# The head of a four-layer kernel: first row tile centred only for its v products, second row's statistics on ScalarE, norms interleaved, buffers cleared later on GpSimd

## The chip, the cores and the metric

One Trainium2 chip, one of its cores. The time is the device time of one execution in microseconds, and the median over runs is what counts. A core has five engines with instruction queues of their own: TensorE (PE, with a separate path for weight loads, PEld), VectorE (DVE), ScalarE (ACT), GpSimd (POOL) and SyncE (SP), which mostly issues transfers. Each runs its own queue in order and waits on semaphores for the others. Row tiles of 128 rows lie across the partitions; TensorE writes to PSUM, and VectorE or ScalarE copies from there to SBUF ("evacuates").

## The reference

Four layers A, B, A, B on x of 2048 x 576 in bf16, each with a residual. Only the first layer's beginning is touched by the change.

```python
def _layernorm(x, axis=-1, eps=1e-05):
    m = jnp.mean(x, axis=axis, keepdims=True)
    v = jnp.var(x, axis=axis, keepdims=True)
    return (x - m) / jnp.sqrt(v + eps)

def _A_ref(x, wqkv, wo):
    qkv = (x @ wqkv).reshape(B, S, 3, H, Dh).transpose(2, 0, 3, 1, 4)
    q, k, v = qkv[0], qkv[1], qkv[2]
    ...
    logits = jnp.einsum('bhsd,bhswd->bhsw', q, kg) * scale
    attn = _softmax(logits, axis=-1)
    o = jnp.einsum('bhsw,bhswd->bhsd', attn, vg)
    return o.transpose(0, 2, 1, 3).reshape(B, S, D) @ wo

x = x + _A_ref(_layernorm(x), A_wqkv, A_wo)
x = x + _B_ref(_layernorm(x), B_w_in, B_w_sp, B_b_sp, B_w_out)
...
```

## The kernel before, in words

The kernel runs the layers in turn (`build_kernel`). In layer A the engines' orders are written out by hand (`tc.manual_schedule` over PE, ACT, DVE, POOL and SP): the order of the Python statements is each engine's queue.

The first layer has a head of its own (`li == 0`, from line 676). Rows are taken in a permuted order (`rows_of`: first even rows, then odd), in 16 row tiles, here called rows 0 to 15.

- Loads (lines 687 to 693): row 0 on SP's queue, row 1 on ScalarE's, rows 2 and 3 on SP's, then the weights for v (`wv_sb`), rows 4 to 7, the weights for q and k (`wqk_sb`), rows 8 to 11. `exp_table` loads ScalarE's table for the exponential.
- Warm-up: 46 matmuls of a 128x128 identity with itself (L699).
- `build_window_rows` makes constant rows that give the attention window. It returns four pieces: `part0` (VectorE: bits of the row numbers), `pads` (GpSimd clears `win_pat`), `part1` (VectorE, and two transfers to DRAM), `part2` (GpSimd: four small operations and one transfer to DRAM). `load_pat` brings the pattern back from DRAM (four transfers on SP), and `fill_window_rows` spreads it over QK (VectorE, L201 and L204).
- Line 703 writes a column of ones into `v_ext` on ScalarE (each head has 18 values of v and a 1, from which the softmax's denominator comes). `setup_bufs` clears the last columns of four exponential buffers `P_sb` and four output buffers `o_t` on GpSimd (L434, L436).

A row tile's norm consists of `B_` (two `bn_stats` on VectorE, L715), `G_` (`bn_aggr`: mean and variance, L718), `R_` (VectorE adds epsilon, L727; GpSimd raises to -0.5, L728) and `A_` (VectorE: subtract the mean, multiply by the reciprocal deviation, into one of four buffers `ln_xn` taken in turn, L735). For rows 0 to 3 `T_pe` transposes the normed tile on TensorE (five transposes of 128x128 into a PSUM tile `pt`, L742), and ScalarE copies it into `xnT` (L745; in two pieces for row 0). From row 4 on, `T_` lets SP issue a transposing transfer instead.

`VW(t, hh, dve)` computes half a row tile of v: five matmuls into a PSUM tile `pv` (L451) and an evacuation into `v_ext` (L443 on VectorE, L445 on ScalarE). The v tiles are those of the attention: tile 0 has rows 0 to 127 of the permuted order, tile t begins 8 rows before its 120 queries, so that tile 1 needs the last 8 columns of row tile 0 in `xnT` and all but a few of row tile 1. Below, "(t, h)" is half h of tile t.

The head's order on TensorE is: warm-up, transposes of row 0, (0,0), row 1, (0,1), row 2, (1,0), (1,1), (2,0), row 3, (2,1), (3,0), (3,1); on VectorE the statistics of row i + 1 stand ahead of the norm of row i. The loop that writes this out:

```python
S_(0)
R_(0, 1)
for i in range(3):
    B_(i + 1)
    A_(i)
    G_(i + 1)
    R_(i + 1, 1)
    T_pe(i)
    for t, hh in (((0, 0),), ((0, 1),), ((1, 0), (1, 1)))[i]:
        VW(t, hh, False)
```

Then the q/k products follow (`PG`, `PG_mm`, L462): for each 128 columns d of q or k and each 512 rows cc, five matmuls of 512 columns, evacuated by ScalarE into `stg` buffers; once a buffer is complete, transfers on GpSimd's and SP's queues scatter it over QK by heads (L78). The ten (d, cc) with cc = 0 and 1 come first, cc = 1 needing rows 4 to 7. After them come (4,0) to (7,1) of v, eight more q/k products, and between these the first score group (`L_mm(0)`, L536) with its exponentials (`EXP`, L545).

PSUM tiles of these kinds are taken in turn from five places (`PT_tile`, two tagged Y and three PT); a tile's place must have been evacuated before it is taken again.

Of the kernel before, what the change touches and what calls it, by code (L numbers as in the profile page):

```python
# [9 lines left out]
ACT = mybir.ActivationFunctionType  # L10
ALU = mybir.AluOpType
AX = mybir.AxisListType
f32 = mybir.dt.float32
# [5 lines left out]
P = 128  # L19
D = 576  # L20
H = 32
DH = 18
# [4 lines left out]
EPS = 1e-5  # L27
# [36 lines left out]
class K:  # L64
# [316 lines left out]
    def layer_A(self, li):  # L381
        nc, tc, cfg = self.nc, self.tc, self.cfg
        S, NT, XW, NS = cfg.S, cfg.NT, cfg.XW, cfg.NS
        scale = float(DH ** -0.5)
# [43 lines left out]
        def k0_(t):  # L428
            return cfg.tiles[t][2]


        def setup_bufs(eng):
            for pb in P_bufs:
                eng.memset(pb[:, :, :, QT:P], 1.0)  # L434
            for ob_ in o_bufs:
                eng.memset(ob_[:, D:640], 0.0)  # L436
# [4 lines left out]
        def evac(out, in_, dve):  # L441
            if dve:
                nc.vector.tensor_copy(out=out, in_=in_)  # L443
            else:
                nc.scalar.copy(out=out, in_=in_)  # L445

        def VW(t, hh, dve):
            nk = tdim(t)[0]
            pv = self.PT_tile([P, 512], f32, "pv")
            for c in range(5):  # L450
                nc.tensor.matmul(pv[:nk, 0:288], lhsT=self.xnT[:, c, k0_(t):k0_(t) + nk],  # L451
                                 rhs=wv_sb[:, c, hh * 288:(hh + 1) * 288], start=(c == 0), stop=(c == 4))
            evac(v_ext[:nk, t, 16 * hh:16 * hh + 16, 0:DH], pv[:nk, 0:288].rearrange("p (b d) -> p b d", d=DH), dve)

        stg_tiles, stg_left = {}, {}
        dma_rr, stg_rr = [0], [0]
# [219 lines left out]
        if li == 0:  # L676
# [18 lines left out]
            self.zero_right()  # L695
            self.make_ident()
            warm = self.PT_tile([P, 512], f32, "warm")
            for _ in range(46):
                nc.tensor.matmul(warm[:, 0:P], lhsT=self.ident[:], rhs=self.ident[:], start=True, stop=True)  # L699
# [3 lines left out]
            nc.scalar.copy(out=v_ext[:, :, :, DH:DH + 1], in_=self.ones[:, None, None, :].to_broadcast([P, NT, H, 1]))  # L703
            rows[0]()
            rows[1]()
            setup_bufs(nc.gpsimd)
            mvs = sb.tile([P, NS, 2], f32, name="lnx_mv", tag="lnx_mv", bufs=1)
            rstds = sb.tile([P, NS], f32, name="lnx_rstd", tag="lnx_rstd", bufs=1)

# [2 lines left out]
            def B_(i):  # L712
                sts[i] = st = sb.tile([P, 2, nc.vector.BN_STATS_DIM], f32, name="ln_st", tag="ln_st", bufs=3)
                for s in range(2):
                    nc.vector.bn_stats(out=st[:, s, :], in_=xts[i][:, s * 288:(s + 1) * 288])  # L715

            def G_(i):
                nc.vector.bn_aggr(out=mvs[:, i, :], in_=sts.pop(i)[:])  # L718

            def S_(*tiles):  # L720
                for i in tiles:
                    B_(i)
                    G_(i)

            def R_(i0, n):
                rs = rstds[:, i0:i0 + n]
                nc.vector.tensor_scalar_add(out=rs, in0=mvs[:, i0:i0 + n, 1], scalar1=EPS)  # L727
                nc.gpsimd.tensor_tensor(out=rs, in0=rs, in1=self.neg_half[:, 0:1].to_broadcast([P, n]), op=ALU.pow)  # L728
            xns = {}

            def A_(*tiles):
# [3 lines left out]
                    nc.vector.tensor_scalar(out=xn[:, 0:D], in0=xts[i], scalar1=mvs[:, i, 0:1],  # L735
                                            scalar2=rstds[:, i:i + 1], op0=ALU.subtract, op1=ALU.mult)

            def T_pe(i):
                xn = xns.pop(i)
                pt = self.PT_tile([P, 5, P], bf16, "pt")  # L740
                for c in range(5):
                    nc.tensor.transpose(pt[:, c, :], xn[:, c * P:(c + 1) * P], self.ident[:])  # L742
                r = i * P
                for c0, c1 in ((0, 3), (3, 5)) if i == 0 else ((0, 5),):
                    nc.scalar.copy(out=self.xnT[:, c0:c1, r:r + P], in_=pt[:, c0:c1])  # L745

            def T_(*tiles):
                for i in tiles:
                    self.ln_T(xns.pop(i), i * P, P)
            S_(0)  # L750
            R_(0, 1)
            for i in range(3):
                B_(i + 1)
                A_(i)
                G_(i + 1)
                R_(i + 1, 1)
                T_pe(i)
                for t, hh in (((0, 0),), ((0, 1),), ((1, 0), (1, 1)))[i]:
                    VW(t, hh, False)
            rows[2](nc.sync)  # L760
            A_(3)
            VW(2, 0, False)
            T_pe(3)
            VW(2, 1, False)
            VW(3, 0, False)
            VW(3, 1, False)
            x3 = sb.tile([P, 4, D], bf16, name="x_in3", tag="x_in", bufs=2)
            x_load(x3[:], 12, 4, nc.sync)
            stgs.append(x3[:].rearrange("p a b -> p (a b)")[:, 0:2 * CBW].rearrange("p (a b) -> p a b", a=2))
# [12 lines left out]
            R_(8, 4)  # L782
            S_(12)
            A_(8, 9, 10, 11)
            T_(8, 9, 10, 11)
# [483 lines left out]
```

## Time and profile before

| | us |
|---|---|
| median of 3 runs | 1152.9 (1152.79 to 1153.15) |
| profiled execution | 1152.74, of which its span is 1150.9 |
| TensorE busy | 1142.6 (99% of the span) |
| VectorE, ScalarE, GpSimd busy | 539.7, 370.5, 259.6 |
| first warm-up matmul starts | 1.36 |
| first transposes of a normed row start | 6.00 |
| first v product starts | 7.03 |
| first q/k product starts | 13.42 |

How to read the lines below. A line of a timeline gives start, length, engine, line, operation, output <- input, shapes and count, and in brackets the idle time before it with what released it; instructions of a kind that follow each other are merged. A line of the chain gives start, length and what ran in the chain that ended last. A line of the groups gives count, busy time and mean length in ns, then the idle time before them. A line of a stretch gives its bounds and length, then busy time and count of PE, PEld, DVE, ACT and POOL, the granted clock, the share of the DMA engines and GB/s. In a list of transfer queues stand packets, MB and share.

### The profile page before, as it was taken

Reading aid. Unit: us, or ns where it says so; the run is one execution under the profiler, and the core shown is the slowest. Engines: PE = TensorE matmul, PEld = TensorE weight load, DVE = VectorE, ACT = ScalarE, POOL = GpSimd, SP = SyncE. Lnnn points to the kernel's source line nnn. Section 1 sums busy time; section 2 is a strip of 40 time slices with the busy share of each in tenths; the row PEclk is TensorE's granted clock in tenths of the full one; section 3 lists DMA queues with packets and bytes.
Section 4 is the critical chain, followed back from the end, with each engine's and each line's share of the span. In section 5 each row is a group of like instructions: output and inputs, shape, how many; then the busy total and the mean of one; then the engine's idle time right before and its main releaser. Section 6 shows DMA issues by size and latency. Waiting matters only on the chain.

```text
span 1150.9 us, 29693 instructions
## 1 busy us (share of the span) xinstructions
PE 1142.6 (99%) x12930; PEld 614.5 (53%) x12949; DVE 539.7 (47%) x1198; ACT 370.5 (32%) x660; POOL 259.6 (23%) x387
## 2 busy tenths in 40 slices
PE   8999999999999999999999999999999999999998
PEld 5567554444444444457755775544444444444676
DVE  8789987312233222244466889843322223222312
ACT  5589565011111111102247876541111111011000
POOL 3689654000000000002153767530000000000000
PEclk9999999999999999999999999999999999999999
DMA  8877696000000000049455867920000000001322
GB/s 195 183 164 200 141 211 137 10 13 13 13 1 13 13 13 2 1 152 213 110 110 110 180 152 176 246 60 1 13 13 13 13 13 1 13 2 30 101 74 58
DMA packets 177372, 91.26 MB, mean 79 GB/s; under 512 B 128788, under 2 KB 170420, under 8 KB 177242
## 3 DMA queue, kind: packets, MB, share of 16 engines
q1 hardware_dynamic: 164762, 70.75, 28.1%
q0 software_dynamic: 5888, 12.72, 4.6%
q10 hardware_dynamic: 6592, 5.90, 1.7%
q8 instruction: 101, 1.65, 0.6%
q14 instruction: 29, 0.24, 0.1%
HBM read 35.46 MB, written 14.69 MB: 44 GB/s over the span
## 4 chain that ended last, share of the span: by engine, by line
PE 97%; ACT 1%; DVE 1%; issue 0%; DVEq 0%; ACTq 0%
PE hh L234 79%; PE pp L462 6%; PE pv L451 3%; PE pw L629 3%; PE O_ps L559 3%; PE L_ps L536 2%; ACT P_sb L545 1%; PE L_ps L462 1%; PE hh L1191 0%; PE pt L595 0%; DVE ln_st L715 0%; DVE ln_xn L735 0%; DVE win_bits L158 0%; ACT v_ext L445 0%; ACT xnT L745 0%
## 5 line engine op out<-in xcount | busy, mean ns | idle before, releaser
L234 PE MATMUL hh<-Wq,Z 64*128 64x512 bf16 x4608 | 505.8, 376 | 0.0
L234 PEld LDWEIGHTS <-Z 64*128 64x128 bf16 x6984 | 339.8, 94 | 310.1
L1095 DVE TENSOR_TENSOR g_tmp<-hh,ln_xn 128x512 f32<-128x512 f32 x144 | 92.8, 686 | 452.3 <-PE hh L234 452.3
L947 ACT COPY bank_turn<-ones 1x1 bf16<-1x1 bf16 x239 | 44.8, 188 | 538.5 <-PE hh L234 538.5
L78 POOL DMA_DIRECT2D wout<-in_B_w_out_dram x4 | 4.3, 1075 | 602.0 <-PE hh L234 602.0
L234 PE MATMUL hh<-wout,Z 64*128 64x288 bf16 x2232 | 137.0, 283 | 0.0
L545 ACT ACTIVATE P_sb<-L_ps 128x1440 bf16<-128x1440 f32 (+3 forms) x136 | 125.0, 971 | 24.6 <-PE L_ps L536 23.2
L234 PE MATMUL hh<-xnT,w 64*128 64x512 bf16 x1152 | 132.2, 376 | 0.0
L234 PE MATMUL hh<-win2a,xnT 64*128 64x512 bf16 (+1 forms) x960 | 118.7, 355 | 0.0
L234 PEld LDWEIGHTS <-xnT 64*128 64x128 bf16 x1440 | 69.9, 94 | 70.0 <-issue 0.5
L1020 DVE BATCH_NORM_STATS2 z_st<-zp 128x6 f32<-128x512 bf16 (+1 forms) x160 | 93.0, 624 | 13.0 <-ACT zp L1018 12.9
L1086 ACT ACTIVATE z1T<-hh 128x1024 bf16<-128x1024 f32 x72 | 73.7, 1024 | 61.9 <-PE hh L234 61.9
L234 PEld LDWEIGHTS <-w 64*128 64x128 bf16 x1152 | 56.1, 94 | 68.3
L1096 DVE TENSOR_TENSOR Z<-g_tmp,z1T 128x512 bf16<-128x512 f32 x144 | 92.4, 683 | 0.0
L1018 ACT ACTIVATE zp<-hh 128x1024 bf16<-128x1024 f32 (+1 forms) x96 | 76.1, 810 | 48.8 <-PE hh L234 48.6
L462 PE MATMUL pp<-xnT,wqk_sb 128*128 128x512 bf16 (+1 forms) x313 | 74.2, 379 | 0.9
L234 PE MATMUL hh<-win2b,xnT 64*128 64x512 bf16 (+1 forms) x480 | 72.8, 355 | 0.0
L1160 DVE TENSOR_TENSOR x_new<-hh,xo 128x288 bf16<-128x288 f32 x64 | 26.3, 453 | 93.0 <-PE hh L234 85.0
L299 POOL TENSOR_SCALAR ln_xn<-x_new,ln_mv,ln_rstd 128x576 bf16<-128x576 bf16 x28 | 64.2, 2293 | 2.7
L78 POOL DMA_DIRECT2D QK<-stg x76 | 48.0, 636 | 36.5 <-DVE stg L443 21.9
L462 PEld LDWEIGHTS <-wqk_sb 128*128 128x128 bf16 (+1 forms) x360 | 32.1, 97 | 36.6 <-issue 1.9
L1044 POOL TENSOR_SCALAR Z<-zp,z_mv,z_rstd 128x256 bf16<-128x256 bf16 x32 | 50.7, 1584 | 3.5
(124 smaller groups left out, 753.3 us busy)
## 6 DMA issues: line engine op xcount, KB each, us to landing
xres<-x_new SPq DMA_DIRECT2D x44, 144.0 KB
wout<-in_B_w_out_dram POOLq DMA_DIRECT2D x4, 1296.0 KB, 7.4
xo<-xres SPq DMA_DIRECT2D x32, 144.0 KB
xn_rows<-ln_xn SPq DMA_DIRECT2D x28, 160.0 KB
w<-in_B_w_in_dram SPq DMA_DIRECT2D x16, 256.0 KB
QK<-stg POOLq DMA_DIRECT2D x51, 72.0 KB, 4.4
QK<-stg SPq DMA_DIRECT2D x37, 72.0 KB
xo<-in_A_x_dram SPq DMA_DIRECT2D x6, 288.0 KB
```

The lines of the kernel that those rows point to most:

```text
L78: return eng.dma_start(out=out, in_=in_)
L234: ins = self.nc.tensor.matmul(outs[a_], lhsT=lhs(a_, c, r0), rhs=rhs(a_, c, r0), start=start and k_ == 0, stop=stop and k_ == len(chunks) ...
L299: e.tensor_scalar(out=xn[:nrows, 0:D], in0=x_t[:nrows, :], scalar1=mv[:nrows, 0:1], scalar2=rstd[:nrows, 0:1], op0=ALU.subtract, op1=ALU.mult)
L462: nc.tensor.matmul(pp, lhsT=w, rhs=self.xnT[r0:r1, c, cc * 512:(cc + 1) * 512], start=start, stop=stop, tile_position=(r0, 0))
L545: nc.scalar.activation(out=P_bufs[2 * jp + s % 2][:nk, :, :, 0:nq], in_=Lv[:nk, :, :, 0:nq], func=ACT.Exp, scale=scale)
L947: self.turn_on = lambda tok: nc.scalar.copy(out=tok, in_=self.ones[0:1, 0:1])
L1018: nc.scalar.activation(out=zp[:, w0:w0 + n], in_=pz, func=ACT.Gelu_apprx_tanh)
L1020: nc.vector.bn_stats(out=st[:, x // 512, :], in_=zp[:, x:x + min(512, w0 + n - x)])
L1044: eng.tensor_scalar(out=Z[:, b0:b1, i, :], in0=zv[:, b0:b1, :], scalar1=mv[:, 0:1], scalar2=rstd[:, 0:1], op0=ALU.subtract, op1=ALU.mult)
L1086: lambda ht, z1T=z1T, q2=q2: nc.scalar.activation(out=z1T[:, q2 * 512:(q2 + 2) * 512], in_=ht[:].rearrange("p a b -> p (a b)"), func=ACT.G ...
L1095: nc.vector.tensor_tensor(out=tmp[:], in0=pg[:, a_, :], in1=bsp[:, qs], op=ALU.add)
L1096: nc.vector.tensor_tensor(out=uT(jj)[:, sub, qs], in0=tmp[:], in1=z1Ts[jj, sub][:, qs], op=ALU.mult)
```

## The change

- Warm-up of 40 instead of 46 matmuls.
- Row 0: VectorE writes the centred row (mean subtracted, not scaled) into `ln_xn` 0 (`xc`). It is transposed, copied in two pieces into `o_slot` 0 (`xcT`), and both halves of v's tile 0 are computed from it; ScalarE's evacuation multiplies by row 0's reciprocal deviation (`scaled`). Afterwards row 0 is normed, transposed and copied to `xnT` as before, first its last 8 columns, then the other 120 (`T_out`).
- Row 1's statistics: two passes on ScalarE (sum; sum of squares of the differences from the mean), GpSimd computes mean, variance and power. VectorE's `bn_stats` and `bn_aggr` of row 1 are gone.
- The order on TensorE becomes: warm-up, centred row 0, (0,0), row 0, row 1, (0,1), (1,0), row 2, (1,1), (2,0), row 3, (2,1), (3,0), (3,1). ScalarE copies row 3 (and row 2) before it evacuates (2,0) (and (1,0)).
- `pads` moves on GpSimd behind the power of row 2, `part2` ahead of the powers of rows 4 to 7. The ones in `v_ext` and `setup_bufs` move behind the power of rows 8 to 11, the ones from ScalarE to GpSimd.
- The statistics of row 6 move ahead of the norms of rows 4 and 5 on VectorE, those of row 8 ahead of the norms of rows 6 and 7.

```diff
-        def VW(t, hh, dve):
+        def VW_mm(t, hh, xT=None):
             nk = tdim(t)[0]
             pv = self.PT_tile([P, 512], f32, "pv")
             for c in range(5):
-                nc.tensor.matmul(pv[:nk, 0:288], lhsT=self.xnT[:, c, k0_(t):k0_(t) + nk],
+                nc.tensor.matmul(pv[:nk, 0:288], lhsT=self.xnT[:, c, k0_(t):k0_(t) + nk] if xT is None else xT[:, c, 0:nk],
                                  rhs=wv_sb[:, c, hh * 288:(hh + 1) * 288], start=(c == 0), stop=(c == 4))
-            evac(v_ext[:nk, t, 16 * hh:16 * hh + 16, 0:DH], pv[:nk, 0:288].rearrange("p (b d) -> p b d", d=DH), dve)
+            return v_ext[:nk, t, 16 * hh:16 * hh + 16, 0:DH], pv[:nk, 0:288].rearrange("p (b d) -> p b d", d=DH)
+
+        def VW(t, hh, dve):
+            evac(*VW_mm(t, hh), dve)
...
-            for _ in range(46):
+            for _ in range(40):
...
-            nc.scalar.copy(out=v_ext[:, :, :, DH:DH + 1], in_=self.ones[:, None, None, :].to_broadcast([P, NT, H, 1]))
             rows[0]()
-            rows[1]()
-            setup_bufs(nc.gpsimd)
...
+            def E_(i0, n):
+                nc.vector.tensor_scalar_add(out=rstds[:, i0:i0 + n], in0=mvs[:, i0:i0 + n, 1], scalar1=EPS)
+
+            def W_(i0, n):
+                rs = rstds[:, i0:i0 + n]
+                nc.gpsimd.tensor_tensor(out=rs, in0=rs, in1=self.neg_half[:, 0:1].to_broadcast([P, n]), op=ALU.pow)
+
             def R_(i0, n):
...
+                E_(i0, n)
+                W_(i0, n)
...
-            def T_pe(i):
-                xn = xns.pop(i)
+            def T_mm(xn):
                 pt = self.PT_tile([P, 5, P], bf16, "pt")
                 for c in range(5):
                     nc.tensor.transpose(pt[:, c, :], xn[:, c * P:(c + 1) * P], self.ident[:])
-                r = i * P
-                for c0, c1 in ((0, 3), (3, 5)) if i == 0 else ((0, 5),):
-                    nc.scalar.copy(out=self.xnT[:, c0:c1, r:r + P], in_=pt[:, c0:c1])
+                return pt
+
+            def T_out(i, pt, c0=0, c1=5, r0=0, r1=P):
+                nc.scalar.copy(out=self.xnT[:, c0:c1, i * P + r0:i * P + r1], in_=pt[:, c0:c1, r0:r1])
...
+            def scaled(out, in_):
+                nc.scalar.activation(out=out, in_=in_, func=ACT.Identity, scale=rstds[:, 0:1])
+            sums = sb.tile([P, 2], f32, name="lnx_sum", tag="lnx_sum", bufs=1)
+            spill = self.xn_bufs[1][:, 0:D]
+            nc.scalar.activation(out=spill, in_=xts[1], func=ACT.Identity, accum_out=sums[:, 0:1])
+            nc.gpsimd.tensor_scalar(out=mvs[:, 1, 0:1], in0=sums[:, 0:1], scalar1=1.0 / D, scalar2=None, op0=ALU.mult)
+            nc.scalar.activation(out=spill, in_=xts[1], func=ACT.Square, scale=-1.0, bias=mvs[:, 1, 0:1],
+                                 accum_out=sums[:, 1:2])
             S_(0)
-            R_(0, 1)
-            for i in range(3):
-                B_(i + 1)
-                A_(i)
-                G_(i + 1)
-                R_(i + 1, 1)
-                T_pe(i)
-                for t, hh in (((0, 0),), ((0, 1),), ((1, 0), (1, 1)))[i]:
-                    VW(t, hh, False)
-            rows[2](nc.sync)
-            A_(3)
-            VW(2, 0, False)
-            T_pe(3)
-            VW(2, 1, False)
+            E_(0, 1)
+            xc = self.xn_bufs[0]
+            nc.vector.tensor_scalar(out=xc[:, 0:D], in0=xts[0], scalar1=mvs[:, 0, 0:1], scalar2=None, op0=ALU.subtract)
+            W_(0, 1)
+            nc.gpsimd.tensor_scalar(out=rstds[:, 1:2], in0=sums[:, 1:2], scalar1=1.0 / D, scalar2=EPS,
+                                    op0=ALU.mult, op1=ALU.add)
+            W_(1, 1)
+            B_(2)
+            pt = T_mm(xc)
+            xcT = o_slots[0]
+            for c0, c1 in ((0, 3), (3, 5)):
+                nc.scalar.copy(out=xcT[:, c0:c1], in_=pt[:, c0:c1])
+            scaled(*VW_mm(0, 0, xcT))
+            A_(0)
+            G_(2)
+            R_(2, 1)
+            rows[1]()
+            A_(1)
+            pt0 = T_mm(xns.pop(0))
+            T_out(0, pt0, r0=P - 8)
+            pt = T_mm(xns.pop(1))
+            T_out(1, pt)
+            v01 = VW_mm(0, 1, xcT)
+            scaled(*v01)
+            T_out(0, pt0, r1=P - 8)
+            B_(3)
+            G_(3)
+            E_(3, 1)
+            A_(2)
+            W_(3, 1)
+            for i in (1, 2):
+                v0 = VW_mm(i, 0)
+                if i == 2:
+                    rows[2](nc.sync)
+                    A_(3)
+                pt = T_mm(xns.pop(i + 1))
+                T_out(i + 1, pt)
+                evac(*v0, False)
+                VW(i, 1, False)
             VW(3, 0, False)
             VW(3, 1, False)
+            rows[3](nc.gpsimd)
...
             S_(4, 5)
             R_(4, 2)
+            S_(6)
             A_(4, 5)
             T_(4, 5)
-            S_(6, 7)
+            S_(7)
             R_(6, 2)
-            rows[3](nc.gpsimd)
+            S_(8)
             A_(6, 7)
             T_(6, 7)
-            S_(8)
             self.load_pat(nc.sync)
             S_(9, 10, 11)
             R_(8, 4)
+            nc.gpsimd.memset(v_ext[:, :, :, DH:DH + 1], 1.0)
+            setup_bufs(nc.gpsimd)
             S_(12)
```

More of the change, by code (lines that the diff above doesn't have):

```diff
@@ L723, in S_ @@
                     G_(i)
+            def E_(i0, n):
[3 more added lines that the diff above has]
+                nc.gpsimd.tensor_tensor(out=rs, in0=rs, in1=self.neg_half[:, 0:1].to_broadcast([P, n]), op=ALU.pow)
             def R_(i0, n):
-                rs = rstds[:, i0:i0 + n]
-                nc.vector.tensor_scalar_add(out=rs, in0=mvs[:, i0:i0 + n, 1], scalar1=EPS)
-                nc.gpsimd.tensor_tensor(out=rs, in0=rs, in1=self.neg_half[:, 0:1].to_broadcast([P, n]), op=ALU.pow)
+                E_(i0, n)
+                W_(i0, n)
             xns = {}
```

## The prediction

> **What bounds the kernel now.** I read the page's head first, then busy time by stretch, then the chain that ended last.
>
> ```profile
> span 1150.9 us, 29693 instructions
> PE 97%; ACT 1%; DVE 1%; issue 0%; DVEq 0%; ACTq 0%
> 0.00:13.42 13.42, 10.54 (x106) 8.70 (x107) 11.13 (x49) 9.09 (x15) 6.78 (x36) 1.00 0.91 258
> 13.42:50.00 36.58, 36.29 (x230) 18.68 (x232) 29.17 (x66) 18.42 (x32) 18.38 (x31) 1.00 0.78 147
> ```
>
> The columns after the length are PE, its weight loads, DVE, ACT, POOL, granted clock, DMA share, GB/s. From 13.42 us TensorE is busy 36.29 of 36.58 us; 13.42 us is when the first q/k product (L462) starts. Everything that the change edits in TensorE's order lies before it. So the question is one number: when does the first q/k product start afterwards? Each 0.1 us there is 0.1 us at the end, as long as nothing later becomes late. The first 13.42 us are not bound by one engine, so I read the chain through them.
>
> ```profile
> 4.82 0.73 DVE ln_st L715 x2
> 5.54 0.40 DVE ln_xn L735
> 5.94 0.13 DVE lnx_mv L718
> ...
> 6.10 0.15 DVE lnx_rstd L727
> ...
> 8.38 0.38 DVE ln_xn L735
> ...
> 8.81 0.45 PE pt L742 x5
> 9.26 1.85 PE pv L451 x15
> ...
> 11.54 0.60 ACT xnT L745
> ...
> 12.18 1.40 PE pv L451 x10
> 13.58 0.22 PE pp L462
> ```
>
> Up to 8.76 us it is VectorE: statistics and norms of rows 0 to 2 in turn, without a gap. Then it is TensorE (row 2 transposed, three v products), ScalarE's copy of row 3, and the last two v products. The timelines of TensorE and ScalarE give the pieces that I build with:
>
> ```profile
> 5.13 0.22 PE L699 MATMUL warm<-ident 128*128 128x128 bf16 x1
> 6.00 0.45 PE L742 MATMUL pt<-ident,ln_xn 128*128 128x128 bf16 x5 [0.65 <-DVE ln_xn L735]
> 7.03 0.79 PE L451 MATMUL pv<-wv_sb,xnT 128*128 128x288 bf16 x5 [0.57 <-ACT xnT L745]
> 7.65 0.44 PE L742 MATMUL pt<-ident,ln_xn 128*128 128x128 bf16 x5
> 7.93 0.78 PE L451 MATMUL pv<-wv_sb,xnT 128*128 128x288 bf16 x5
> 10.94 0.44 PE L742 MATMUL pt<-ident,ln_xn 128*128 128x128 bf16 x5
> 12.18 1.40 PE L451 MATMUL pv<-wv_sb,xnT 128*128 128x288 bf16 x10 [0.19 <-ACT xnT L745]
> 13.42 1.46 PE L462 MATMUL pp<-xnT,wqk_sb 128*128 128x512 bf16 x5
> 7.85 0.40 ACT L445 CAST v_ext<-pv 128x288 bf16<-128x288 f32 x1 [0.60 <-PE pv L451]
> 9.30 0.69 ACT L745 COPY xnT<-pt 128x640 bf16<-128x640 bf16 x1
> 11.43 0.70 ACT L745 COPY xnT<-pt 128x640 bf16<-128x640 bf16 x1
> ```
>
> One v product (five matmuls) holds TensorE 7.65 - 7.03 = 0.62 us, one row's transposes 7.93 - 7.65 = 0.28 us. Norm ready to transposes: 6.00 - 5.94 = 0.06. First row's transposes to its first v product, with the copy in two pieces: 7.03 - 6.00 = 1.03. A whole row's round trip, transposes to a v product that reads the copy: 12.18 - 10.94 = 1.24. Last two v products: 13.42 - 12.18 = 1.24.
>
> **The change part by part.** *First row.* VectorE now centres row 0 right after its variance is closed, so neither the power of -0.5 on GpSimd nor the 0.73 us of row 1's statistics lie ahead of it: centred at 4.82 + 0.40 = 5.22 instead of 5.94. Gain so far 0.72 us. Transposes start at 5.28, the first v product at 6.31. The six warm-up matmuls that go (ends at 5.35 now) would have stood in front of those transposes.
>
> *The price of it.* Row 0 must still be normalised, transposed and copied for the q/k products: one more VectorE norm (0.40), five more transposes (0.28), a copy more on ScalarE. And the new order interleaves: transposes of row 1, its copy, then v product (1,0), then transposes of row 2, and so on, each next transpose standing behind a v product that waits for the previous row's copy. Following TensorE: first v product 6.31; row 0's transposes again 6.93; row 1's transposes 7.21; v product (1,0) a round trip later, 8.45 (v product (0,1) of 0.62 runs inside the wait); row 2's transposes 9.07; (2,0) a round trip later, 10.31; row 3's transposes 10.93; (3,0) 12.17; first q/k product 12.17 + 1.24 = 13.41. Three round trips of 1.24 us, each with only 0.28 + 0.62 of own work, replace the wait for VectorE: 0.34 us idle three times and 0.28 of added transposes. That gives back nearly the whole 0.72. Result: 13.41 against 13.42.
>
> *Is VectorE in time?* It drops row 1's statistics, mean and epsilon (0.73 + 0.13 + 0.15) and adds the centring. Row 1's norm: 5.22 + 0.73 (row 2's statistics) + 0.40 (row 0's norm) + 0.30 + 0.38 = 7.03, so transposes could start at 7.09; they are due at 7.21: 0.12 spare. Row 2's: 7.03 + 0.73 + 0.30 + 0.38 = 8.44, due 9.07. Row 0's norm writes the buffer that the centred row is read from, so it waits for the transposes (5.28 + 0.45) and for the power (next fence: VectorE's epsilon was done at 4.82, the power follows at once): both over before 5.95.
>
> *Row 1's statistics on ScalarE* take the place of the copy of ones (2.53 us, from 2.58):
>
> ```profile
> L703 ACT COPY v_ext<-ones 128x544 bf16<-128x544 bf16 x1 | 2.5, 2530 | 0.0
> q10 hardware_dynamic: 144, 0.15, 13.2%
> L293 ACT ACTIVATE ln_xn<-x_new,ln_nmr,ln_rstd 128x576 bf16<-128x576 bf16 x15 | 13.0, 868 | 62.3 <-POOL bank_turn L1130 59.0 <-POOL ln_nmr L283 3.3
> L1035 POOL TENSOR_SCALAR z_rstd<-z_mv 128x1 f32<-128x1 f32 x32 | 7.4, 232 | 53.2 <-DVE z_mv L1033 51.3 <-PE hh L234 1.8
> 4.90 0.58 POOL L728 TENSOR_TENSOR lnx_rstd<-lnx_rstd,neg_half 128x1 f32<-128x1 f32 x1 [0.23 <-DVE lnx_rstd L727]
> ```
>
> The second row is row 1's load, the only one on that queue, in a view of the first 3.4 us: all its 144 packets had moved by then. Two passes over 128x576 at 0.87 with GpSimd's mean (0.23) between them: 3.4 + 0.87 + 0.23 + 0.87 and three hand-overs of 0.05 give 5.5, before ScalarE's first copy is due at 5.77. GpSimd then does row 0's power (to 5.48), row 1's variance (to 5.75) and power (to 6.31); row 1's norm asks for it at 6.65. Spare: 0.34, and 0.12 behind it. What the sums cost on ScalarE no row shows: at the least nothing, at the most (a pass doubled) 2 x 0.87 = 1.74, which is 1.3 us past the spare. I take nothing, since a read-out like the engine's shortest rows (0.2 us twice) would still fit.
>
> *Scaled evacuation* of row 0's two v products: between 0.40 (plain, above) and 0.60. It is followed on ScalarE by an 8-column copy and then row 1's copy, which is due at 7.70; the late end moves the path 0.18. I take 0.05. The Trainium skill, "ScalarE: Activation LUTs", section "What ACT_TABLE_LOAD costs", gives about 93 ns for each pointer operand of an ACTIVATE; by that the evacuation is 0.50, an estimate, and the sum moves by at most 0.1.
>
> *Clearing and GpSimd's order.* Eight clears and the ones go behind the power for rows 8 to 11; the pattern's clear goes between the powers of rows 2 and 3; the last window piece, with its transfer, goes ahead of the powers of rows 4 to 7.
>
> ```profile
> L805 DVE MEMSET v_ext<- 128x544 bf16 x1 | 0.5, 512 | 1.8 <-issue 1.8
> 3.86 0.48 POOL L434 MEMSET P_sb<- 128x96 bf16 x4
> 4.28 0.40 POOL L436 MEMSET o_t<- 128x64 bf16 x4
> 13.29 0.77 DVE L735 TENSOR_SCALAR ln_xn<-x_in,lnx_mv,lnx_rstd 128x576 bf16<-128x576 bf16 x2 [0.81 <-POOL lnx_rstd L728]
> 27.20 2.35 DVE L201 COPY QK<-win_pat 128x4096 bf16<-128x4096 bf16 x2
> 28.02 3.40 POOL L78 DMA_DIRECT2D QK<-stg  x4 [5.19 <-DVE QK L204]
> q0 software_dynamic: 18, 0.02, 7.4%
> 48.21 0.44 PE L_ps L536 x16
> ```
>
> They cost 0.51 to 2.53 (by VectorE's and ScalarE's rows for the same 128x544) + 0.88, under the 5.19 us that GpSimd waits before its first scatter: nothing, and without that cover it would push the scatters. The readers are the exponentials behind L536. In the waits for the power that the norms of rows 4 to 7 had (0.81 before the first pair), VectorE now does statistics; that and the earlier window transfer bring SP's row transposes and pattern load forward by one to two us, all of them off TensorE's path. TensorE's first two score groups stand at 42.2 and 48.21; the last GpSimd scatters land before 46 (the q0 row, window 45 to 46), so those have 2 us of slack.
>
> **The sum** on the profiled execution: 1152.74 total (span 1150.9 and 1.84 around it) - 0.01 + 0.05 = 1152.8; it lies 0.16 under the runs' median, so 1152.8 to 1152.9. I say 1152.8.
>
> **The rivals.** *A gain of the packed kind.* If copies overlap better than my round trips, TensorE's own work is the floor: from 6.31, eight v products and four sets of transposes, 8 x 0.62 + 4 x 0.28 = 6.08, so 12.39: 1.03 us earlier, 1151.7. For it: TensorE is idle only 2.88 us of the first 13.42. Against: a whole row's copy took 0.69 and 0.70 here, and each trip has one. *The statistics are late* (slower): ScalarE's sums end so late that row 1's power comes after 6.77. From there each us is one us; the bound above gives +1.3, 1154.1. For it: four engine crossings in series; against: 0.46 spare. *The clearing blocks.* The Trainium skill, "SBUF — State Buffer", section "Who interferes with whom", says GpSimd and VectorE's two-port copies exclude each other for a whole instruction. As a mechanism of this kernel: the clears sit behind VectorE's pattern copies (the L201 row: until 27.20 + 2.35 = 29.55) and with 0.51 + 0.88 of their own end about 31, GpSimd's scatters move 3 us, the last land at 49 instead of 46, and the score group at 48.21 waits 0.9: 1153.7. Against it: the clears are issued before those copies start. *The array slows down.* With fewer warm-up matmuls TensorE could fall back to the pace of its start:
>
> ```profile
> 1.30:2.40 1.10, 1.04 (x11) 1.04 (x11) 1.05 (x4) 1.10 (x1) 0.95 (x6) 1.00 0.47 71
> 4.40:5.40 1.00, 0.95 (x17) 0.77 (x14) 0.95 (x4) 0.71 (x1) 0.77 (x5) 1.00 1.12 319
> ```
>
> 1.04 / 11 = 95 ns against 0.95 / 17 = 56 ns for the same matmul, a factor 1.7, though the granted clock says 1.00 in both. On 6.08 us of work that is up to +4.2: 1157.0. Against: the fast pace was there long before the 40th matmul, and the gap behind it shrinks. This one decides the far side.
>
> **How the numbers follow.** Given back as computed (1152.2 to 1153.3): 0.58. Packed gain (1151.7 to 1152.2): 0.16. Late statistics: 0.11. Blocked clearing: 0.04. Slow array: 0.06. Something unseen: 0.05. The range 1151.7 to 1154.2 leaves out the last two and little else; the likeliest case alone is 1152.2 to 1153.3. Over 0.2% is 2.3 us, about what a measurement of this kernel can tell from no change: no priced gain reaches it, only the unseen (0.03); slower takes the slow array and 0.02; the rest, 0.89, is within.
>
> **What would show it.** The first centred transposes near 5.3, the first v product near 6.3 (right if so); the first q/k product near 13.4 (the sum's test); TensorE idle before (1,0), (2,0) and (3,0), released by xnT copies (the give-back's test); row 1's norm not waiting for GpSimd (statistics in time); GpSimd's clears over before its first scatter. A first q/k product under 12.9 or over 13.9 us would make the prediction wrong, as would a new TensorE wait after it.

## The result and the profile after

| | before | after |
|---|---|---|
| median of 9 runs each, taken together | 1152.9 us (1152.71 to 1153.31) | 1155.6 us (1154.71 to 1156.78) |
| ratio | | 1.0024, 95% interval 1.0014 to 1.0034 |
| profiled execution, its span | 1152.74, 1150.9 | 1155.94, 1154.2 |

The changed kernel is 2.7 us slower (1.6 to 3.9 by the interval). The forecast was 1152.8 with a range up to 1154.2, so the prediction was wrong, and on the side that it held to be unlikely. I read the profile in the order of the prediction's own tests: first the head on TensorE, then what follows it.

TensorE's timeline of the changed kernel, up to the first q/k product (L465 now):

```profile
1.36 4.44 PE L702 MATMUL warm<-ident 128*128 128x128 bf16 x40 [1.36 <-POOL ident L194]
5.60 0.48 PE L747 MATMUL pt<-ident,ln_xn 128*128 128x128 bf16 x5
6.65 0.79 PE L451 MATMUL pv<-wv_sb,o_slot 128*128 128x288 bf16 x5 [0.57 <-ACT o_slot L777]
7.28 0.72 PE L747 MATMUL pt<-ident,ln_xn 128*128 128x128 bf16 x10
8.78 0.79 PE L451 MATMUL pv<-wv_sb,xnT 128*128 128x288 bf16 x5 [0.17 <-ACT xnT L751]
10.63 0.79 PE L451 MATMUL pv<-wv_sb,xnT 128*128 128x288 bf16 x5 [0.17 <-ACT xnT L751]
12.48 1.40 PE L451 MATMUL pv<-wv_sb,xnT 128*128 128x288 bf16 x10 [0.17 <-ACT xnT L751]
13.72 1.46 PE L465 MATMUL pp<-xnT,wqk_sb 128*128 128x512 bf16 x6
```

The structure is the predicted one: the first product 1.05 after the transposes (predicted 1.03), three round trips of 1.85 to 2.13 from one product that reads a copy to the next (predicted 1.86 to 2.14), each ended by ScalarE's copy (L751). The whole is 0.3 us late because the warm-up stood in front of it: its forty matmuls should have been over by 5.28, and held TensorE until 5.60 (the ends of matmuls are modelled). So the q/k products start 0.30 later than before (13.42), and that is a tenth of the loss.

The rest is behind the head. Windows of the changed kernel (bounds and length, then busy time and count of PE, PEld, DVE, ACT, POOL, the granted clock, DMA share, GB/s):

```profile
0.00:13.72 13.72, 11.28 (x106) 9.36 (x107) 11.72 (x50) 9.04 (x20) 8.50 (x35) 1.00 0.90 263
13.72:50.00 36.28, 34.63 (x195) 17.52 (x193) 27.63 (x59) 16.25 (x28) 20.06 (x35) 1.00 0.73 129
```

TensorE is now busy 34.63 of 36.28 us in the stretch in which it had been busy 36.29 of 36.58. The granted clock is 1.00 in both. TensorE's waits in the changed kernel (what waited for what: us in all, times, longest) name what came in:

```profile
PE L_ps L539 <- DVE stg L443: 1.6, 1, 1.6
PE L_ps L539 <- DMA QK<-win2a: 0.8, 2, 0.4
```

Both stand at the first two score groups (L539). To see where they come from I go upstream, VectorE and GpSimd around the clears. Timelines of the changed kernel, and at the end the view of the tile `ln_xn` there (min/median/max in ns):

```profile
17.56 0.82 DVE L715 BATCH_NORM_STATS2 ln_st<-oT 128x6 f32<-128x288 bf16 x2 [2.38 <-DMA oT<-in_A_x_dram]
18.91 0.77 DVE L741 TENSOR_SCALAR ln_xn<-x_in,lnx_mv,lnx_rstd 128x576 bf16<-128x576 bf16 x2 [0.29 <-issue]
...
23.83 4.20 DVE L741 TENSOR_SCALAR ln_xn<-oT,lnx_mv,lnx_rstd 128x576 bf16<-128x576 bf16 x4 [0.16 <-POOL lnx_rstd L730]
27.95 1.21 DVE L201 COPY QK<-win_pat 128x4096 bf16<-128x4096 bf16 x1
...
22.79 1.01 POOL L730 TENSOR_TENSOR lnx_rstd<-lnx_rstd,neg_half 128x4 f32<-128x4 f32 x1 [6.82 <-DVE lnx_rstd L726]
23.75 2.46 POOL L824 MEMSET v_ext<- 128x544 bf16 x1
25.79 0.72 POOL L434 MEMSET P_sb<- 128x96 bf16 x4
26.45 0.40 POOL L436 MEMSET o_t<- 128x64 bf16 x4
31.26 7.43 POOL L78 DMA_DIRECT2D QK<-stg  x11 [4.41 <-ACT stg L445]
...
L741 DVE TENSOR_SCALAR ln_xn<-oT,lnx_mv,lnx_rstd x4: 411/417/3183, 23.8 to 27.6; 128x576 bf16<-128x576 bf16 x4
```

The same places in the kernel before:

```profile
16.97 0.78 DVE L735 TENSOR_SCALAR ln_xn<-x_in,lnx_mv,lnx_rstd 128x576 bf16<-128x576 bf16 x2 [0.81 <-POOL lnx_rstd L728]
22.87 1.45 DVE L735 TENSOR_SCALAR ln_xn<-oT,lnx_mv,lnx_rstd 128x576 bf16<-128x576 bf16 x4 [0.20 <-POOL lnx_rstd L728]
24.71 2.36 DVE L201 COPY QK<-win_pat 128x4096 bf16<-128x4096 bf16 x2 [0.39 <-DMA win_pat<-win_period]
```

Two things happen. The statistics of row 8, now ahead of the norms of rows 6 and 7, wait 2.38 us for the load of rows 8 to 11, so the norms of rows 8 to 11 start at 23.83 instead of 22.87: +0.96. And these four norms take 4.20 us instead of 1.45: the first of them 3.18 instead of about 0.42. GpSimd's clear of the ones starts at 23.75, 0.08 us ahead of that norm; the norm ends at 23.83 + 3.18 = 27.01, and its own 0.41 us began therefore at 26.60, right behind the clears of `P_sb` (25.79 + 0.72 = 26.51): +2.75. Together with the wait for the pattern that before had here (0.39, gone now) this gives 0.96 + 2.75 - 0.39 = 3.32; the pattern copies moved from 24.71 to 27.95, by 3.24.

The remaining way, changed kernel:

```profile
30.34 0.18 DVE L204 COPY QK<-win_pat 128x64 bf16<-128x64 bf16 x1
41.31 1.04 POOL L730 TENSOR_TENSOR lnx_rstd<-lnx_rstd,neg_half 128x4 f32<-128x4 f32 x1
46.16 1.07 POOL L78 DMA_DIRECT2D QK<-win2a  x2 [0.28 <-DMA QK<-stg]
42.39 1.45 DVE L741 TENSOR_SCALAR ln_xn<-x_in,lnx_mv,lnx_rstd 128x576 bf16<-128x576 bf16 x4 [4.08 <-POOL lnx_rstd L730]
43.76 2.48 DVE L443 CAST stg<-pp 128x512 bf16<-128x512 f32 x4
42.68 0.23 PE L539 MATMUL L_ps<-QK 32*128 32x128 bf16 x3
44.49 0.47 PE L539 MATMUL L_ps<-QK 32*128 32x128 bf16 x13 [1.58 <-DVE stg L443]
51.38 0.22 PE L539 MATMUL L_ps<-QK 32*128 32x128 bf16 x1 [0.45 <-DMA QK<-win2a]
51.95 0.23 PE L539 MATMUL L_ps<-QK 32*128 32x128 bf16 x1 [0.34 <-DMA QK<-win2a]
52.11 0.56 PE L562 MATMUL O_ps<-v_ext,P_sb 128*128 128x19 bf16 x16
QK<-win2a POOLq DMA_DIRECT2D x2, 36.0 KB, 5.2
```

and before:

```profile
27.11 0.18 DVE L204 COPY QK<-win_pat 128x64 bf16<-128x64 bf16 x1
37.78 1.04 POOL L728 TENSOR_TENSOR lnx_rstd<-lnx_rstd,neg_half 128x4 f32<-128x4 f32 x1
38.77 4.84 POOL L78 DMA_DIRECT2D QK<-win2a  x8
40.22 1.88 DVE L443 CAST stg<-pp 128x512 bf16<-128x512 f32 x3
42.16 0.40 PE L536 MATMUL L_ps<-QK 32*128 32x128 bf16 x16
48.14 0.40 PE L536 MATMUL L_ps<-QK 32*128 32x128 bf16 x16
48.48 0.56 PE L559 MATMUL O_ps<-v_ext,P_sb 128*128 128x19 bf16 x16
QK<-win2a POOLq DMA_DIRECT2D x2, 36.0 KB, 4.6
```

The last row of each fence is from the list of transfers, for those issued last on GpSimd's queue (us from issue to landing). GpSimd's scatters depend on the pattern copies: the first one starts 0.73 to 0.75 us behind the end of the first L204 copy in each of the twelve traces (27.29 and 28.02 before, 30.52 and 31.26 here), although the profile names ScalarE's `stg` as what ended the wait here. GpSimd's power for rows 12 to 15 is queued behind fifteen scatters. So that power comes 3.53 later (41.31, 37.78), VectorE waits 4.08 for it, and its evacuations of q/k products come 3.54 later (43.76, 40.22). The first of them frees the PSUM place that the score group's fourth matmul takes. From the start of the evacuation to the matmul there are 44.49 - 43.76 = 0.73 us; before, that would have let it go at 40.22 + 0.73 = 40.95, 1.44 us ahead of its time (42.16 + 0.23 = 42.39). TensorE itself reaches it 0.52 later now: 3.54 - 1.44 - 0.52 = 1.58, which is the wait. The second group waits for the last two scatters: 46.16 + 5.2 = 51.36, and the wait ends at 51.38. The first product with v (O_ps) comes at 52.11 instead of 48.48, 3.63 later. Of that, 0.52 was there ahead of the first score group (0.30 of it is the head), the first group adds 1.88 and the second 1.23; the waits named above are 1.58 and 0.79 of these.

### The profile page after: what moved, and what is told of

The parts are those of the page before. It is cut to its first block, busy times and chain, and to the rows that moved or that the text cites. A ratio compares the mean times of both kernels' runs of the same rounds, so it can differ in the third digit from the quotient of the medians.

```text
span 1154.2 us, 29719 instructions
## 1 busy us (share of the span) xinstructions
PE 1145.2 (99%) x12948; PEld 615.4 (53%) x12948; DVE 541.6 (47%) x1195; ACT 370.3 (32%) x665; POOL 263.0 (23%) x390
## 4 chain that ended last, share of the span: by engine, by line
PE 97%; DMA 1%; ACT 1%; POOL 1%; issue 0%; DVE 0%; DVEq 0%; POOLq 0%; ACTq 0%
PE hh L234 79%; PE pp L465 5%; PE pw L632 3%; PE pv L451 3%; PE O_ps L562 3%; PE L_ps L539 2%; POOL QK L78 1%; PE L_ps L465 1%; ACT P_sb L548 1%; DMA QK<-stg 0%; DMA QK<-win2a 0%; PE hh L1234 0%; PE warm L702 0%; PE pt L598 0%; ACT xnT L751 0%
## 5 line engine op out<-in xcount | busy, mean ns | idle before, releaser
L465 PE MATMUL pp<-xnT,wqk_sb 128*128 128x512 bf16 (+1 forms) x330 | 75.4, 379 | 0.0
L1203 DVE TENSOR_TENSOR x_new<-hh,xo 128x288 bf16<-128x288 f32 x64 | 26.3, 453 | 92.6 <-PE hh L234 84.9
L465 PEld LDWEIGHTS <-wqk_sb 128*128 128x128 bf16 (+1 forms) x360 | 32.0, 97 | 36.6 <-issue 2.2
```

Of the source, the lines that this page charges most:

```text
L465: nc.tensor.matmul(pp, lhsT=w, rhs=self.xnT[r0:r1, c, cc * 512:(cc + 1) * 512], start=start, stop=stop, tile_position=(r0, 0))
```

## The experiments

The theory: GpSimd's late clears hold VectorE's norms up, and the scatters pass that on ("the lock"). Its rivals: the 2.38 us wait for the load of rows 8 to 11 is the cause; or the new head is.

*The clears on VectorE.* The changed kernel, with the ones and the eight clears written by VectorE in front of row 8's statistics:

```diff
             R_(6, 2)
+            nc.vector.memset(v_ext[:, :, :, DH:DH + 1], 1.0)
+            setup_bufs(nc.vector)
             S_(8)
...
-            nc.gpsimd.memset(v_ext[:, :, :, DH:DH + 1], 1.0)
-            setup_bufs(nc.gpsimd)
```

> The changed kernel with one edit: the ones in v_ext and the clears of P_sb and o_t are written by VectorE ahead of row 8's statistics, where it waits for a load, instead of by GpSimd behind the power of rows 8 to 11. Theory (GpSimd's clears shut VectorE out of the norms of rows 8 to 11 and so push the pattern copies, the scatters and the first two score groups): the norm of row 8 falls from 3.18 us to about 0.43, the pattern copies start near 25.2 instead of 27.95, the first scatter near 28.5 instead of 31.26, TensorE's waits before the two score groups (1.58 and 0.79) go, and the median falls by 2 to 2.5 us to about 1153.3. Rival (row 8's statistics, moved ahead, wait 2.4 us for their load, and that is the cause): norms still start a us late, the scatters stay near 30 or later and the median falls by less than 1 us.

Ratio 1.0006 (0.9997 to 1.0015). VectorE's timeline of this kernel:

```profile
23.82 1.45 DVE L741 TENSOR_SCALAR ln_xn<-oT,lnx_mv,lnx_rstd 128x576 bf16<-128x576 bf16 x4 [0.16 <-POOL lnx_rstd L730]
25.18 2.35 DVE L201 COPY QK<-win_pat 128x4096 bf16<-128x4096 bf16 x2
```

The four norms start where they started (23.82), and take 1.45 again. Most of the loss is gone although these norms are as late as in the changed kernel. (The clears, and 1.85 us of "issue" ahead of them, fill the time in which VectorE had waited for the load.)

*Row 8's statistics back behind the norms of rows 6 and 7*, clears as in the changed kernel:

```diff
             S_(7)
             R_(6, 2)
-            S_(8)
             A_(6, 7)
             T_(6, 7)
+            S_(8)
```

> The changed kernel with one edit: row 8's statistics stand behind the norms of rows 6 and 7 again. Theory of the clears: the 2.4 us wait for the load moves behind those norms but the power of rows 8 to 11 is hardly earlier, since it needs row 8's load all the same; the norm of row 8 is still about 3.2 us, the first scatter comes at 30.3 to 31.3, the median is 1154.5 to 1155.6. Rival (the wait for the load is the cause): first scatter near 28.5, median near 1153.3.

Ratio 1.0010 (1.0001 to 1.0019). The four norms still take 3.97, but they start at 21.39, and the pattern copies at 25.28. My expectation failed in part: the power came 2.45 us earlier (20.34 instead of 22.79) and the first scatter at 28.59, where the rival had put it, and the median of 1154.37 lies just under the 1154.5 to 1155.6 that I had forecast. So the place of row 8's statistics has a share as well; the two delays add up on one path.

*Both edits together*, VectorE's clears now between `T_(6, 7)` and `S_(8)`:

> Both edits together: clears on VectorE ahead of row 8's statistics, and these behind the norms of rows 6 and 7. Under either theory the late part of the loss is gone: no wait before the first two score groups, first q/k product near 13.7 as in the changed kernel, median 1153.0 to 1153.5, that is the 0.3 us that the head itself lost. If the median stays above 1154.5, neither is the cause.

Ratio 1.0015 (1.0006 to 1.0024): a miss. The clears on VectorE had lain inside the load's wait in the first experiment. Here they stand on VectorE's path: the norms of rows 8 to 11 start at 24.53 and the pattern copies at 25.90, later than with either edit alone. Whether that explains the whole 1.0015 isn't shown: a kernel below, with the pattern copies at 25.65, loses nothing that is clear of the noise. The median of 1154.29 stays under the 1154.5 that would have spoken against both causes. The profiled execution (1156.76) was this kernel's slowest, with a granted clock of 0.97 from 50 to 100 us, so its length isn't used.

*The other way round: the kernel before, with the late clears alone.*

```diff
-            nc.scalar.copy(out=v_ext[:, :, :, DH:DH + 1], in_=self.ones[:, None, None, :].to_broadcast([P, NT, H, 1]))
...
-            setup_bufs(nc.gpsimd)
...
             R_(8, 4)
+            nc.gpsimd.memset(v_ext[:, :, :, DH:DH + 1], 1.0)
+            setup_bufs(nc.gpsimd)
```

> The kernel before with one part of the change alone: the ones in v_ext go from ScalarE to GpSimd, and they and the clears stand behind the power of rows 8 to 11. Theory of the clears: row 8's norm takes about 3.2 us instead of 0.43, the pattern copies start near 27.2 instead of 24.71, the first scatter near 30.5 instead of 28.02, TensorE waits 0.5 to 1.5 us before the first score groups, and the median rises by 1 to 2 us to 1154 to 1155. Rival (head or load wait is the cause): no change, 1152.9.

Ratio 1.0022 (1.0012 to 1.0031), nearly the whole loss, with the old head and the old place of row 8's statistics. GpSimd, VectorE and TensorE of this kernel:

```profile
22.64 2.44 POOL L781 MEMSET v_ext<- 128x544 bf16 x1
22.72 4.21 DVE L733 TENSOR_SCALAR ln_xn<-oT,lnx_mv,lnx_rstd 128x576 bf16<-128x576 bf16 x4 [0.20 <-POOL lnx_rstd L726]
26.85 2.35 DVE L201 COPY QK<-win_pat 128x4096 bf16<-128x4096 bf16 x2
43.84 0.47 PE L536 MATMUL L_ps<-QK 32*128 32x128 bf16 x13 [1.12 <-DVE stg L443]
```

The same norms of 4.21 behind the same clear, and the same wait for the evacuation. Neither rival is in this kernel, so neither is needed: the late clears are enough for the loss. In the kernel with row 8's statistics back they had cost less (1.0010); there the norms began at 21.39, here at 22.72. The two intervals overlap.

*What is the head worth when the clears cost nothing?* The changed kernel with the eight clears at their old place, the ones on ScalarE behind the head's last evacuation, and row 8's statistics back:

```diff
+            setup_bufs(nc.gpsimd)
...
             VW(3, 1, False)
+            nc.scalar.copy(out=v_ext[:, :, :, DH:DH + 1], in_=self.ones[:, None, None, :].to_broadcast([P, NT, H, 1]))
             rows[3](nc.gpsimd)
```

> The changed head with the clearing where it should cost nothing: P_sb and o_t cleared on GpSimd ahead of row 1's mean, the ones on ScalarE behind the head's last v evacuation, row 8's statistics behind the norms of rows 6 and 7. Theory (two paths end together at the second score group: TensorE's own, first q/k product + 35.1 us, and the scatters, first scatter + 20.8): norms of rows 8 to 11 take 1.45 us together, the pattern copies start near 23, the first scatter near 26.4, no wait for a transfer before the second score group; the time is the head's: first q/k product 13.4 to 14.2, by how long the warm-up matmuls stay slow, median 1152.7 to 1153.5. Rival (the changed head itself costs more than its first q/k product shows): above 1153.8.

Ratio 0.9999 (0.9990 to 1.0008); the first q/k product starts at 13.53. The new head neither gains nor loses more than the interval can tell (1 us either way), as forecast. The pattern copies came at 24.91 where I had put them near 23, because row 8's statistics waited 0.98 us for the load of rows 8 to 11.

*The same with row 8's statistics left ahead* of the norms of rows 6 and 7:

> The same, but row 8's statistics stay ahead of the norms of rows 6 and 7, as in the changed kernel: this is that one move alone. Theory: VectorE waits for the load of rows 8 to 11 (until 16 to 18 us), the norms of rows 6 and 7 start 2 to 3 us later than in the run above, the power of rows 8 to 11 1 to 2 us later, the first scatter near 28, so that the second score group waits up to 0.7 us: median 0 to 0.7 above the run above. Rival (this move is harmless): the same median within 0.3.

Ratio 1.0003 (0.9994 to 1.0012), although VectorE waits 2.73 us for the load. Alone, this move costs nothing that could be measured.

*The kernel before, with the last window piece earlier and the statistics of row 6 ahead of the norms of rows 4 and 5:*

> The kernel before (its head, its clearing) with the harmless part of the change alone: the last window piece ahead of the powers of rows 4 to 7, and row 6's statistics ahead of the norms of rows 4 and 5. Theory: first scatter 1 to 1.8 us earlier than 28.02, first q/k product at 13.4 as before; since TensorE did not wait for the scatters before, no gain from that: 1152.5 to 1152.9. If it is as fast as or faster than the run of the changed head with free clearing, the new head is worth nothing.

Ratio 1.0000 (0.9991 to 1.0009). The pattern copies start at 24.20 and the first scatter at 27.51, both 0.51 earlier than before where I had expected 1 to 1.8, and nothing comes of it.

*The lock at another place.* The free-clears kernel, with the ones on GpSimd right behind the power of rows 4 and 5:

> As the first run of this call, but GpSimd writes the ones behind the power of rows 4 and 5, where VectorE has the norms of rows 4 and 5 next and then statistics. Theory (a GpSimd clear and a two-port VectorE norm shut each other out for a whole instruction, statistics do not): the clear takes about 2.0 to 2.5 us there too; a norm that comes after its start waits for its end (2 us and more), a norm that has begun is not touched, and the statistics run at 0.4 us each as usual. Rival (the norm of row 8 was long for another reason, its buffer or its transfer): norms of rows 4 and 5 at 0.43 each. Median 1153 to 1154.

Ratio 1.0001 (0.9992 to 1.0010). GpSimd and VectorE:

```profile
12.90 2.45 POOL L814 MEMSET v_ext<- 128x544 bf16 x1
13.01 2.84 DVE L742 TENSOR_SCALAR ln_xn<-x_in,lnx_mv,lnx_rstd 128x576 bf16<-128x576 bf16 x2
```

Two norms that take 0.74 in the changed kernel take 2.84 here, behind a clear that started 0.11 us ahead. The lock is there, and it costs nothing: the waits that the free-clears kernel had behind it on VectorE (0.98 us for the load of rows 8 to 11, 0.46 ahead of the pattern copies) are gone, and the pattern copies start at 25.05 instead of 24.91.

*Ones or small clears?* The changed kernel with the ones alone taken to ScalarE behind the head; the eight clears stay late and row 8's statistics stay ahead:

> The changed kernel with the ones alone taken from GpSimd to ScalarE behind the head's last v evacuation; the eight small clears stay behind the power of rows 8 to 11, and the statistics of row 8 stay ahead of the norms of rows 6 and 7. Lock theory (a GpSimd clear that starts first holds VectorE out to its end, so the price is the length of the clears): 0.72 + 0.40 = 1.1 us of clears instead of 3.6, so the norm of row 8 takes 0.8 to 1.5 instead of 3.18, the four norms 1.8 to 2.6 instead of 4.20, pattern copies near 26.3 (27.95 in the changed kernel, 25.65 with no late clears), first scatter near 29.6; ratio about 1.0007 (1.000 to 1.0015). If the small clears do as much as the ones (many short instructions each taking the lock), the pattern copies start at 27.5 or later and the ratio is 1.002.

Ratio 1.0000 (0.9991 to 1.0008): without this one instruction on GpSimd no loss is left that the interval can tell. The first norm took 0.835 instead of 3.18 us, the four 1.85. The pattern copies started earlier than I had expected (24.42 for 26.3) because the load of rows 8 to 11 came 1.2 us earlier in this execution (16.38). The trace alone would leave open whether the early load helped; the ratio stands on all eleven executions, and the kernel above without late clears lost nothing clear either (1.0003) in a trace where the load came at 18.00.

*The ones cleared twice:*

> The changed kernel with the clear of the ones written twice in a row on GpSimd: the suspected cost is doubled. Lock theory, with the scatters co-critical: the norm of row 8 takes 3.18 + 2.46 = 5.6, the pattern copies start near 30.4, the first scatter near 33.7, the last GpSimd scatters end near 49.7, and the first score groups wait another 2.4 us in all: 1158.0 (1157.0 to 1158.6), ratio 1.0044. If the scatters were not what sets the end (the loss sits elsewhere), the time stays at 1155.6, ratio 1.0024.

Ratio 1.0034 (1.0021 to 1.0046), from six executions. That is 0.0010, or 1.2 us, above the changed kernel's ratio where I had expected 2.4 us, but the two intervals overlap, and the two profiled executions have the same span (1154.1 and 1154.2). So it isn't shown that the second clear costs time at the end. What the trace shows is what it does on VectorE:

```profile
22.84 2.46 POOL L824 MEMSET v_ext<- 128x544 bf16 x1
25.35 2.50 POOL L825 MEMSET v_ext<- 128x544 bf16 x1
22.92 6.25 DVE L741 TENSOR_SCALAR ln_xn<-oT,lnx_mv,lnx_rstd 128x576 bf16<-128x576 bf16 x4 [0.16 <-POOL lnx_rstd L730]
```

The four norms take 6.25 us instead of 4.20. I had expected one norm to wait through both clears; none did, as the view of the tile gives 2.71 us as the longest. One norm waited out the first clear (2.53), ran, and the next one waited out the second (2.71).

All versions side by side, from one profiled execution each (us), with the ratio over all runs:

| | pattern copies start | last GpSimd scatter issued | first product with v | span | ratio |
|---|---|---|---|---|---|
| before | 24.71 | 43.61 | 48.48 | 1150.9 | |
| old head, window piece and row 6 moved | 24.20 | 44.02 | 48.81 | 1153.1 | 1.0000 |
| changed, ones on ScalarE | 24.42 | 44.21 | 48.86 | 1150.9 | 1.0000 |
| clears free, row 8 back | 24.91 | 44.50 | 49.03 | 1151.3 | 0.9999 |
| ones on GpSimd behind rows 4 and 5 | 25.05 | 44.31 | 48.98 | 1151.0 | 1.0001 |
| clears on VectorE | 25.18 | 44.42 | 49.56 | 1151.8 | 1.0006 |
| row 8 back | 25.28 | 44.55 | 49.49 | 1151.6 | 1.0010 |
| clears free, row 8 ahead | 25.65 | 45.57 | 49.91 | 1152.1 | 1.0003 |
| clears on VectorE, row 8 back | 25.90 | 45.48 | 51.38 | 1155.0 | 1.0015 |
| before with late clears | 26.85 | 46.14 | 50.38 | 1152.4 | 1.0022 |
| changed | 27.95 | 47.23 | 52.11 | 1154.2 | 1.0024 |
| changed, ones twice | 29.09 | 47.67 | 52.02 | 1154.1 | 1.0034 |

Span minus the start of the first product with v is 1102.0 to 1102.4 in ten of the twelve. The other two have a disturbance of their own: the granted clock of 0.97 named above, and in the old-head kernel a wait of 1.9 us at an L559 matmul for nothing that the profile shows. So what these versions differ by is settled by then, and nothing is made up later. Up to a start of the pattern copies near 25 us the ratio does not move. From 25.2 on it is higher, but at 25.18 and 25.65 (1.0006 and 1.0003) not clear of the noise, so where the slack ends is known only roughly.

No version beat the kernel before by more than the measurement can tell.

## Why the prediction was wrong

- *The head.* Right in structure. The first q/k product was forecast at 13.41; it came at 13.72 here, and at 13.41 to 13.56 in six of the eight experiments that keep the new head (13.97 and 14.20 in the others). These two and the changed kernel's own are the three in which the warm-up took 4.44 or 4.45 us; in the other six it took 3.67 to 4.19. The old head shows the same: 13.42 in the profile before, 13.75 in the two experiments that keep it, whose 46 warm-up matmuls took 5.09. So the 0.30 belongs to the execution, and no run shows that forty matmuls instead of 46 cause it. The packed gain did not occur: ScalarE's copy ended the wait ahead of (1,0), (2,0) and (3,0).
- *Statistics of row 1 and scaled evacuation.* Timelines of ScalarE and VectorE in the changed kernel:

```profile
4.32 0.19 ACT L761 ACTIVATION_READ_ACCUMULATOR ln_xn<-x_in 128x1 f32 x1
7.54 0.50 ACT L758 ACTIVATE v_ext<-pv,lnx_rstd 128x288 bf16<-128x288 f32 x1 [0.67 <-PE pv L451]
6.18 0.43 DVE L741 TENSOR_SCALAR ln_xn<-x_in,lnx_mv,lnx_rstd 128x576 bf16<-128x576 bf16 x1 [0.41 <-POOL lnx_rstd L770]
6.88 0.43 DVE L741 TENSOR_SCALAR ln_xn<-x_in,lnx_mv,lnx_rstd 128x576 bf16<-128x576 bf16 x1
```

  The statistics were in time for TensorE: row 1's norm (6.88) has no wait, and the transposes of rows 0 and 1 (7.28) have no idle time before them. They were later than the sum, though. ScalarE's first pass began at 3.73, where I had put 3.4, the end of the load's last packet; and VectorE's wait of 0.41 ahead of row 0's norm ended with GpSimd's variance of row 1 (L770), a wait that the prediction did not have. The read-out of a sum, which had no row before, is an instruction of its own of 0.19 us, and the guess of 0.2 us twice fits. The scaled evacuation took 0.50 (0.40 plain), inside the bounds of 0.40 and 0.60. The 93 ns for a pointer operand that the Trainium skill gives ("ScalarE: Activation LUTs", "What ACT_TABLE_LOAD costs") agree with that.
- *The slow array.* In part: the change of pace came later within the warm-up and gave the 0.30, up to 0.79 in the first experiment (14.20), where the first transposes were still slow too (0.74 instead of 0.48). The later round trips ran at the fast pace, so it never came near the 4.2 us of the rival.
- *Clearing: the step that failed.* "They cost 0.51 to 2.53 (by VectorE's and ScalarE's rows for the same 128x544) + 0.88, under the 5.19 us that GpSimd waits before its first scatter: nothing". The length was in the bounds (3.10 from the first start to the last end, for 1.39 to 3.41), and GpSimd's own cover was real: it still waited 4.41 us before its first scatter. But the sum priced only the engine on which the clears run. The cost fell on another engine, VectorE, whose norms were next and could not run beside them: 2.75 us there, and the scatters were late through VectorE, not through GpSimd.
- *The rival that named the lock* quoted the right rule and put it the wrong way round: it let the clears wait behind VectorE's pattern copies, and then dismissed it with "the clears are issued before those copies start". That is just what makes them win. The Trainium skill ("SBUF — State Buffer", "Who interferes with whom") says that whoever issues first gets the shared ports for the whole instruction and that the other blocks; the traces agree (3.18, 2.84 and 2.71 us for a norm or a pair behind a clear of 2.45). I did not ask which VectorE instructions of that kind follow right behind the power: the norms of rows 8 to 11, released by the same power behind which the clears stand.
- *"So those have 2 us of slack."* Wrong by most of its size. I took the time when the queue's last packets had moved (45 to 46) for the landing that TensorE waits for. By the list of transfers, the last two scatters take 4.6 us from issue to landing; the second of them starts about 0.5 ahead of 43.61, so by estimate it lands near 47.7, 0.4 ahead of the group at 48.14. The other way, through the power queued behind the scatters and the evacuations, had 1.44 us, and the prediction didn't see it at all. With the 2 us, even a delay of 3 us would have cost only 1.
- *"Forward by one to two us"* for the row transposes and the pattern load: they did not move. SP's transposes of rows 4 and 5 start at 14.00 (14.03 before), its pattern load at 22.08 (21.81). What VectorE saved in front of rows 6 and 7 it lost in the wait for the load of rows 8 to 11, whose arrival I had not looked up.

What stays open: why single executions of one kernel spread by 2 to 4 us where the scatters are late (1154.85 to 1159.44 with the ones twice) and whether that differs from the kernel before, which spread by 0.6 us in the nine runs beside the changed kernel but by 1.3 to 4.2 in the 16 to 33 beside the experiments. The load of rows 8 to 11 comes between 16.4 and 18.0 us in the executions in which VectorE waits for it, and may be part of it; each kernel has only one trace, so this wasn't shown.

## What to carry to other kernels

A piece of work that is moved "into an idle stretch" of GpSimd has to be priced on VectorE too: look up which VectorE instruction starts next, and whether the two can run at once. A short instruction that waits behind a long one pays the long one's remainder, and an engine that is off the critical path can be the one that pays. Slack has to be taken at the waiting end, from the instruction that would wait and the landing that it waits for, and along each way that leads there, with what is queued in order behind the delayed transfers.

## What the runs showed of the hardware that was not expected

- The time at which the warm-up reaches the fast pace differs between executions: forty matmuls took from 3.67 to 4.45 us, forty-six 3.99 us once and 5.09 twice, though the granted clock there is 1.00.
- Writing a value of 2 bytes into every 38th byte (the ones, 128x544) took 2.44 to 2.50 us on GpSimd and 2.53 to 2.56 on ScalarE; GpSimd's clear of 128x528 without gaps took 0.53. On VectorE the row says 0.51, but 1.8 to 1.9 us of "issue" stand ahead of it, in the first and third experiment as in the later layer of the kernel before; whether that time belongs to the clear isn't shown.
- A waiting VectorE instruction gets in between two of GpSimd's clears of 2.5 us (ones written twice), but in the changed kernel it did not get in between the ones and the four short clears of `P_sb` behind them. What decides that was not tried.
